# Turning the attention output of the last step on TensorE in place of a transposing DMA

## The chip, the core and the metric

The kernel runs on one core of a Trainium2 chip. The core has five engines that work side by side, each through its own list of instructions in order: TensorE (PE; its weight loads are shown apart as PEld), VectorE (DVE), ScalarE (ACT), GpSimd (POOL) and SyncE (SP), which here only issues DMAs. They meet through semaphores. The metric is the device time of one execution in microseconds (us), lower being better.

## What is computed

Attention for 4 batches, 8 heads, 768 positions and 64 elements a head, followed by a feed-forward layer with a maximum of three products:

```
scores = q @ k.T / sqrt(64)
mask   = causal                                   for retrieval heads
mask   = causal and (key < 4 or distance < 64)    for the others
a      = softmax(scores where mask else -1e9)
x      = (a @ v), its heads laid side by side     # 3072 x 512
h      = max(x @ w1, x @ w2, x @ w3)              # 3072 x 768
out    = h @ w_out                                # 3072 x 512
```

Inputs and output are float32; the kernel computes its products in float16 with float32 sums.

## The kernel before, in words

**Tiling.** The rows of a batch are cut into two halves of 384 positions. One step, t, is one batch, one half and one group of four heads (`qd`): 4 x 2 x 2 = 16 steps, t = 0 to 15, with `where(t)` giving batch, half and group. Step 15 is the last: batch 3, second half, heads 4 to 7. A step has two pairs of heads, i = 0 and 1.

**Stages of a step.** `scores` multiplies q and k into PSUM (line 441) and takes the exponential on ScalarE (line 452); `masks` multiplies by the mask, mostly on POOL. `av(t, i)` multiplies the result with v for one pair: 60 small products for the two pairs of a second-half step, 30 each (line 495), into one PSUM bank `oacc`. VectorE then takes the reciprocal of the sums (line 503) and scales into `x`, float16, positions on partitions (line 505). The feed-forward layer needs this turned, features on partitions: tile `xT[b, half][hp]`, hp being the pair's number from 0 to 3 in its batch.

**Two ways to turn x.** Which one a step takes is told by the tuple `BY_DMA` (line 89):

- If t is in it, `av` itself issues a transposing DMA on SP's queue from x to xT (line 514), right after x is made.
- If not, `av` keeps x, and a later call `turn_x(t, i)` transposes its three 128 x 128 blocks on TensorE into a PSUM bank named `tr` (line 527) and copies that to xT, on VectorE unless told otherwise (line 531).

In both cases `turn_x` of a half's last pair puts the feed-forward of that half into `queue`. Before the change steps 0, 1 and 3 are turned by TensorE, all others by DMA.

**The feed-forward** `ffn(b, half)` is a generator that hands out lots of work. There are 18 lots of four products of 384 columns (line 338: three weights for each of six output blocks), each followed by a copy on ScalarE (line 346) or a maximum on VectorE (line 349), the third maximum writing `hT`; and then, for each of three row blocks, six products with `w_out` (line 364), a copy out of PSUM (line 370), and a DMA of the result (line 371). A row block counts for two turns of the generator. Results of products sit in a ring of four PSUM banks (`bkp`, one bank each for `yy`, `oacc` and `tr`); the last feed-forward takes every second one from the pool of `scores` instead (named `yst`).

**What sets the order.** The order is written out by hand (`ctx.enter_context(tc.manual_schedule())`). The list `PROGRAM` has one row for each part of a step's scores: a number of lots of feed-forward to weave in, a flag, and four strings of calls; the loop at its end runs the first string, the scores, the second string, about half of the lots by `fill`, the third string, the rest of the lots, and the fourth string. Its last three rows, for which no scores are left, are

```
(3.94, False, "v 15 1 ap", "x 14 1", "", "av 15 0, x 15 0"),
(3.94, False, "", "av 15 1", "", ""),
(3.94, False, "x 15 1", "", "", ""),
```

where `av 15 0` is `av(15, 0)` and `x 15 0` is `turn_x(15, 0)`. Thus `x 15 0` directly follows `av 15 0` with nothing woven between, `av 15 1` comes next, and `x 15 1` follows the lots that are woven in after it. When the list ends, the last feed-forward runs alone.

Of the kernel before, what the change touches and what calls it, by code (L numbers as in the profile page):

```python
# [51 lines left out]
def kernel(  # L52
# [33 lines left out]
    NQ = H // G  # L86
    NT4 = B * 2 * NQ

    BY_DMA = (2, 4, 5, 6, 7, 8, 9, 10, 11, 12, 13, 14, 15)

    consts = ctx.enter_context(tc.tile_pool(name="consts", bufs=1))
    stage = ctx.enter_context(tc.tile_pool(name="stage", bufs=3))
# [390 lines left out]
    def av(t, i):  # L483
# [25 lines left out]
        if hp == 0:  # L509
            xT[b, half] = [  # L510
                xtp.tile([P, HB, P], FP16, tag=f"xT{n}", name=f"xT{n}") for n in range(KS)
            ]
        if t in BY_DMA:
            nc.sync.dma_start(
# [5 lines left out]
    def turn_x(t, i, op=None):  # L520
        b, half, qd = where(t)
        hp = 2 * qd + i
        if t not in BY_DMA:
            x = xs.pop((t, i))
# [202 lines left out]
```

## Time and profile before

| what | value |
|---|---|
| median of 6 runs | 202.04 us (201.52 to 202.25) |
| profiled execution | 201.88 us |
| its span (first to last instruction recorded) | 200.0 us |
| TensorE busy | 188.7 us (94%) |
| VectorE busy | 123.2 us (62%) |
| ScalarE busy | 131.6 us (66%) |
| POOL busy | 122.5 us (61%) |
| transposing DMAs, line 514 | 26, median 2.4 us from issue to landing |
| turns by TensorE, line 527 | 18 blocks, 0.22 us each, overlapping |
| copies of turned blocks by VectorE, line 531 | 4, median 0.34 us |

A row of the timeline gives the start in us from the span's start, the length, the engine, the line, the operation with output and input, and how many instructions are merged into it; in square brackets stands how long the engine sat idle before it and whose result ended the wait. Matmuls overlap, so a row's length is that of the whole group, and one product alone shows a longer time than its share of a group. A row of the chain of work that ended last gives start, length and what held the chain.

### The profile page before, as it was taken

The page shows a single profiled execution, that of the slowest core. Times are in us where ns is not written, and L with a number is a line of the kernel's source. Part 1 is how long each engine was busy: PE and PEld are TensorE (multiplying, and loading weights), DVE is VectorE, ACT ScalarE, POOL GpSimd, SP SyncE. Part 2 cuts the span into 40 slices and gives each one's busy share as a digit, 9 for nine tenths or more (in the row PEclk, how much of TensorE's full clock was granted, in tenths as well). Part 3 has the DMA queues.
Part 4 walks back from the last instruction along what each step waited for, and adds up shares of the span by engine and source line. Part 5 has one row for each costly group of instructions (what it writes and reads, how often), then busy time and mean ns, then how long its engine had stood idle before and what let it go on. Part 6 is the DMA issues. An engine that isn't in the chain of part 4 may idle for free.

```text
span 200.0 us, 5133 instructions
## 1 busy us (share of the span) xinstructions
PE 188.7 (94%) x2059; PEld 109.0 (55%) x2059; DVE 123.2 (62%) x242; ACT 131.6 (66%) x206; POOL 122.5 (61%) x153
## 2 busy tenths in 40 slices
PE   7797998896999999999999999999999999999992
PEld 2355654454566466574555565575555565755552
DVE  2798687999777839871554649961555234443540
ACT  4586798597875777666787685848768769313221
POOL 3599169479896905787969635699947547500000
PEclk9999999999999999999999999999999999999999
DMA  6999999997729892804359995502401240023004
GB/s 182 269 222 245 278 236 214 209 211 177 174 52 167 161 260 94 169 11 141 98 90 142 176 247 126 100 20 86 134 20 23 105 75 20 3 57 141 3 0 157
DMA packets 43245, 26.48 MB, mean 132 GB/s; under 512 B 33558, under 2 KB 38230, under 8 KB 43222
## 3 DMA queue, kind: packets, MB, share of 16 engines
q1 hardware_dynamic: 37206, 15.01, 34.4%
q0 software_dynamic: 4784, 10.23, 26.3%
q10 hardware_dynamic: 1232, 0.92, 1.4%
q8 instruction: 16, 0.26, 0.6%
q14 instruction: 7, 0.06, 0.1%
HBM read 25.17 MB, written 6.29 MB: 157 GB/s over the span
## 4 chain that ended last, share of the span: by engine, by line
PE 74%; DMA 10%; POOL 6%; DVE 3%; issue 2%; ACT 2%; SPq 1%; DVEq 0%; ACTq 0%; POOLq 0%
PE yy L338 39%; PE yy L364 13%; PE st L441 10%; PE oacc L495 9%; DMA vs<-in_v_dram 6%; PE yst L338 3%; DMA ks<-in_k_dram 2%; DVE KQ L190 2%; ACT pt L452 1%; DMA out_dram<-ot 1%; POOL vs L208 1%; POOL qs L126 1%; POOL ks L126 1%; PE yst L364 1%; ACT ot L370 1%
## 5 line engine op out<-in xcount | busy, mean ns | idle before, releaser
L479 POOL TENSOR_TENSOR pt<-pt,mk 128x512 f16<-128x512 f16 (+1 forms) x76 | 80.4, 1081 | 37.2 <-ACT pt L452 37.1
L452 ACT ACTIVATE pt<-st 128x1024 f16<-128x1024 f32 (+3 forms) x99 | 83.1, 894 | 21.1 <-PE st L441 20.3
L349 DVE TENSOR_TENSOR acc<-yy,acc 128x384 f16<-128x384 f32 x45 | 25.1, 558 | 28.1 <-PE yy L338 18.4
L338 PE MATMUL yy<-xT,w2t 128*128 128x384 f16 x180 | 35.9, 327 | 1.7 <-DVE hT L349 1.7
L338 PE MATMUL yy<-xT,w1t 128*128 128x384 f16 x180 | 36.1, 327 | 0.1
L338 PE MATMUL yy<-xT,w0t 128*128 128x384 f16 x180 | 35.6, 326 | 0.4 <-DVE xT L531 0.4
L346 ACT CAST acc<-yy 128x384 f16<-128x384 f32 x45 | 21.0, 484 | 17.1 <-PE yy L338 10.6
L364 PE MATMUL yy<-woutt,hT 128*128 128x512 f16 (+1 forms) x138 | 32.0, 375 | 0.0
L441 PE MATMUL st<-KQ 32*128 32x384 f16 (+4 forms) x560 | 28.5, 279 | 0.6 <-DVE KQ L190 0.5
L349 DVE TENSOR_TENSOR hT<-yy,acc 128x384 f16<-128x384 f32 x45 | 24.9, 559 | 6.7 <-PE yy L338 4.3
L495 PEld LDWEIGHTS <-pt 128*128 128x128 f16 x672 | 23.9, 97 | 5.4 <-issue 2.2
L338 PEld LDWEIGHTS <-w2t 128*128 128x128 f16 x192 | 17.6, 98 | 15.2 <-issue 4.0
L190 DVE STREAM_TRANSPOSE KQ<-kq 128x384 f32<-128x384 f32 x24 | 25.7, 1131 | 0.0
L338 PEld LDWEIGHTS <-w0t 128*128 128x128 f16 x192 | 18.2, 98 | 12.9 <-issue 1.0
L495 PE MATMUL oacc<-va,pt 128*128 128x65 f16 x352 | 24.8, 193 | 0.3 <-ACT va L392 0.3
L338 PEld LDWEIGHTS <-w1t 128*128 128x128 f16 x192 | 17.3, 98 | 12.5 <-issue 1.3
L370 ACT COPY ot<-yy 128x512 f32<-128x512 f32 x22 | 12.9, 587 | 15.5 <-PE yy L364 9.3
L495 PE MATMUL oacc<-vf,pt 128*128 128x65 f16 x320 | 21.1, 193 | 0.9 <-POOL vf L394 0.9
L364 PEld LDWEIGHTS <-hT 128*128 128x128 f16 x150 | 13.9, 98 | 14.5 <-issue 0.3
L441 PEld LDWEIGHTS <-KQ 32*128 32x128 f16 (+1 forms) x560 | 12.2, 93 | 17.3 <-issue 11.8
L505 DVE TENSOR_TENSOR x<-oacc,rc 128x384 f16<-128x384 f32 x32 | 17.8, 557 | 1.3 <-DVE rc L503 0.2
L503 DVE RECIPROCAL rc<-oacc 128x6 f32<-128x6 f32 x32 | 6.1, 191 | 20.1 <-PE oacc L495 19.8
(71 smaller groups left out, 129.0 us busy)
## 6 DMA issues: line engine op xcount, KB each, us to landing
out_dram<-ot SPq DMA_DIRECT2D x23, 256.0 KB, 2.9
vs<-in_v_dram SPq DMA_DIRECT2D x21, 256.0 KB, 6.0
kq<-in_k_dram POOLq DMA_DIRECT2D x6, 384.0 KB, 5.4
kq<-in_q_dram POOLq DMA_DIRECT2D x6, 384.0 KB, 7.6
qs<-in_q_dram ACTq DMA_DIRECT2D x4, 192.0 KB, 3.8
ks<-in_k_dram SPq DMA_DIRECT2D x4, 192.0 KB, 3.6
w0t<-in_moe_w_dram POOLq DMA_DIRECT2D x1, 768.0 KB, 7.4
ks<-in_k_dram POOLq DMA_DIRECT2D x2, 384.0 KB, 6.8
```

The costliest lines, as they stand in the source:

```text
L190: nc.vector.transpose(out=dst.rearrange("c (p j) -> c j p", j=n)[:, j0:j1], in_=src.rearrange("c (j i) -> c j i", i=R),)
L338: nc.tensor.matmul(yy[:, 0:HALF], w_t[wi][:, ks, ni * P : (ni + 1) * P], xT[b, half][ks].rearrange("p a t -> p (a t)"), start=(ks == 0), s ...
L346: nc.scalar.copy(out=acc[ni], in_=yy[:, 0:HALF])
L349: nc.vector.tensor_tensor(out=dst, in0=yy[:, 0:HALF], in1=acc[ni], op=ALU.max)
L364: nc.tensor.matmul(yo[:, 0:n], hT[ns][:, tb * P : (tb + 1) * P], woutt[:, ns, c : c + n], start=(ns == 0), stop=(ns == NNB - 1),)
L370: op(out=ot[:, c : c + n], in_=yo[:, 0:n])
L441: nc.tensor.matmul(sts[g // m][:, g % m, c0 : c0 + n * P], KQ[rows, 0, ki * P : (ki + 1) * P], KQ[rows, 1, t0 : t0 + n * P], start=(c0 == ...
L452: nc.scalar.activation(out=pts[t, i][:, u, h0 : h0 + m, 0:w], in_=st[:, :, 0:w], func=AF.Exp, scale=sc,)
L479: engine.tensor_tensor(out=x, in0=x, in1=m, op=ALU.mult)
L495: nc.tensor.matmul(o[:, qi, hl, 0 : D + 1], pt[:, u, hl, c : c + P], vv[:, 2 * hp + hl, ki, 0 : D + 1], start=(idx == 0), stop=(idx == len ...
L503: nc.vector.reciprocal(out=rc, in_=o[:, :, :, D])
L505: nc.vector.tensor_tensor(out=x, in0=o[:, :, :, 0:D], in1=rc.unsqueeze(3).to_broadcast([P, HB, 2, D]), op=ALU.mult,)
```

## The change

The step t = 15 is taken out of `BY_DMA`. Its two transposing DMAs are no longer issued, and the two calls `turn_x(15, 0)` and `turn_x(15, 1)`, which until now did nothing on TensorE for this step, turn x there and copy it to xT on VectorE. The rows of `PROGRAM` stay as they are.

```diff
-    BY_DMA = (2, 4, 5, 6, 7, 8, 9, 10, 11, 12, 13, 14, 15)
+    BY_DMA = (2, 4, 5, 6, 7, 8, 9, 10, 11, 12, 13, 14)
```

The code on which it acts, unchanged, in `av` and in `turn_x`:

```
        if t in BY_DMA:
            nc.sync.dma_start(out=xT[b, half][hp], in_=x.rearrange(...), transpose=True)
        else:
            xs[t, i] = x
...
        if t not in BY_DMA:
            x = xs.pop((t, i))
            tr = bank([P, 1024], FP16, "tr")
            for qi in range(HB):
                nc.tensor.transpose(tr[:, qi * P : (qi + 1) * P], ...)
            (op or nc.vector.tensor_copy)(out=xT[b, half][hp]..., in_=tr[:, 0:HALF])
```

## The prediction

> **What bounds the kernel now.** I read the page's span and its chain of work that ended last first, to know which engine sets the end:
>
> ```profile
> span 200.0 us, 5133 instructions
> PE 74%; DMA 10%; POOL 6%; DVE 3%; issue 2%; ACT 2%; SPq 1%; DVEq 0%; ACTq 0%; POOLq 0%
> ```
>
> TensorE holds three quarters of the chain. What matters is whether it holds it where the change is made, so next comes the chain in order of time, cut to 172 to 182 us (start, length, what), where the step of t = 15 lies:
>
> ```profile
> 171.97 1.79 PE yy L338 x11
> 173.76 1.87 PE oacc L495 x60
> 175.63 1.30 PE yy L338 x8
> 176.93 3.89 PE yy L364 x18
> 180.82 0.65 PE yst L338 x4
> ```
>
> Every piece begins where the one before it ends: no gap. The 60 products are the two calls av(15, 0) and av(15, 1). From there to the last product TensorE is the chain, at a granted clock of 1.00 in each stretch that I asked for. So any time that the change makes TensorE spend or wait there goes whole into the end.
>
> The third view is the timeline of the same moments. First TensorE's matmuls (start, length; lines left out are like their neighbours):
>
> ```profile
> 174.47 0.22 PE L495 MATMUL oacc<-va,pt 128*128 128x65 f16 x2
> 174.53 0.22 PE L495 MATMUL oacc<-vf,pt 128*128 128x65 f16 x2
> ...
> 175.47 0.81 PE L338 MATMUL yy<-xT,w1t 128*128 128x384 f16 x4
> 176.12 0.81 PE L338 MATMUL yy<-xT,w2t 128*128 128x384 f16 x4
> 176.77 4.05 PE L364 MATMUL yy<-woutt,hT 128*128 128x512 f16 x18
> 180.66 0.65 PE L338 MATMUL yst<-xT,w0t 128*128 128x384 f16 x3
> ```
>
> Counting 30 products from 173.60, the first call's last one is in the row at 174.47 and ends at 174.69; the second call starts at 174.53 with no pause. Then VectorE:
>
> ```profile
> 174.73 0.20 DVE L503 RECIPROCAL rc<-oacc 128x6 f32<-128x6 f32 x1 [0.95 <-PE oacc L495]
> 174.96 0.56 DVE L505 TENSOR_TENSOR x<-oacc,rc 128x384 f16<-128x384 f32 x1
> 175.67 0.20 DVE L503 RECIPROCAL rc<-oacc 128x6 f32<-128x6 f32 x1
> 176.10 0.56 DVE L505 TENSOR_TENSOR x<-oacc,rc 128x384 f16<-128x384 f32 x1 [0.23 <-DVE rc L503]
> 176.58 0.55 DVE L349 TENSOR_TENSOR acc<-yy,acc 128x384 f16<-128x384 f32 x1
> 177.23 0.56 DVE L349 TENSOR_TENSOR hT<-yy,acc 128x384 f16<-128x384 f32 x1
> ```
>
> x of (15, 0), what is to be turned, is ready at 174.96 + 0.56 = 175.52 us. While VectorE makes it, TensorE already runs the second call. That is the whole point of the case.
>
> Last, what a turn by TensorE costs, from steps that are turned so already (line 527), out of two stretches of the timeline:
>
> ```profile
> 15.68 0.33 PE L527 MATMUL tr<-ident,x 128*128 128x128 f16 x3
> ...
> 15.85 0.35 PE L495 MATMUL oacc<-va,pt 128*128 128x65 f16 x6
> ...
> 49.19 0.34 PEld L527 LDWEIGHTS <-x 128*128 128x128 f16 x6 [0.94 <-DVE x L505]
> 49.19 0.51 PE L527 MATMUL tr<-ident,x 128*128 128x128 f16 x6 [0.65 <-DVE x L505]
> ```
>
> Three turns hold TensorE from 15.68 to 15.85, 0.17 us; six in a row give (0.51 - 0.22)/5 = 0.058 us each, 0.22 being the length of one, so again 0.17 for three. The last two rows also show a turn waiting for x: the product that it waits for ended at 48.58 + 0.56 = 49.14 on VectorE, and the load began at 49.19, 0.05 us later.
>
> **What the Trainium skill says.** "TensorE: Matmul & The Clock Gate", Part 3, The mechanism: TensorE may pull weight loads ahead of products in flight, but the products start and end strictly in program order. The trace agrees where it can show it: the third call's products at 15.32 were held 0.29 us for ScalarE's copy of v, and the turn behind them, whose x had been ready since 14.46 + 0.56 = 15.02, did not go ahead; it ran at 15.68, after all of them. Same page, Part 4, PE-mode transpose: a 128x128 turn takes some 275 ns within a kernel, with its result in PSUM, to be copied out. The trace has 0.22 us for one and 0.058 us for each of a row, because they overlap; I use the trace. Same page, Why this matters for your kernels: gaps of TensorE over about 3 us lose the fast clock; the new gap is under 1 us, and after 0.65 us idle at 49.19 the trace's products of 384 columns ran at their usual pace.
>
> **The change, part by part.** (a) Removed: two transposing DMAs on SP's queue, begun at 175.59 and about 176.9. Their bytes moved until about 178.8, and the median from issue to landing over all 26 is 2.4 us. The first product that reads these xT tiles is at 180.66 and follows the one before it without a gap. Gain: 0. SP's next duty, the output at 178.93, waits for ScalarE (12.6 us, in SP's waits), not for these. The queue is never the limit, and the output is issued no earlier.
>
> (b) "x 15 0" stands right after "av 15 0" with no filling between, and "av 15 1" opens the next line. So TensorE's order becomes 30 products, 3 turns, 30 products. The turns cannot start before x: 175.52 + 0.05 = 175.57. The second call then starts at 175.57 + 0.17 = 175.74 in place of 174.53: +1.21 us, of which 0.17 is work and 1.04 is time in which TensorE used to do the second call's products. Behind the waiting turn stands everything that TensorE has left; no other engine has work to bring forward in this stretch (POOL ended at 172.5, ScalarE and VectorE only serve TensorE).
>
> (c) "x 15 1" stands after the fill that follows av(15, 1). Two lots of line 338 and one lot of line 364 (six products, 6 x 0.216 = 1.30 us) run first. Its turns come at 176.77 + 1.21 + 1.30 = 179.28; its x is ready at 176.66 + 1.21 = 177.87, so 1.4 us of cover hide the wait; uncovered, it would cost what (b) does, some 1.2. Three turns, again +0.17 us. The lots of line 364 are only regrouped, 6 and 12 rather than 18.
>
> (d) Two copies from PSUM on VectorE, 0.34 us each (line 531, median). The first runs at about 175.95 to 176.29, before the second reciprocal, due at 175.67 + 1.21 = 176.88: cover 0.59. The second ends near 180.0, and the first product that wants it is at 182.04: cover 2.0. Cost 0; without cover 0.34 each.
>
> (e) Two PSUM banks more in a ring of four. The first turn takes one free since 173.13, the second that of the second call, free at 177.87. The first lot of line 364 takes the first turn's (free 176.29, wanted 177.98); the next two take banks whose readers end by 179.00, wanted at 179.45 and later. The closest cover is 0.4 us. Cost 0; a late copy there would cost its lateness, at most about 0.3.
>
> (f) The loads of hT for line 364 are just in time today (0.33 us of idle weight loading, but 18 products in 4.05 us is (4.05 - 0.375)/17 = 0.216 each, the normal pace). All of that chain moves by the same 1.21, so nothing is added.
>
> Sum: 1.21 + 0.17 = 1.38 us. The profiled execution took 201.88 us (span 200.0 and 1.88 around it), so 203.26; the median of the runs is 0.16 higher, so 203.4.
>
> What the trace doesn't show is this turn between these two calls. Bounds: 0.34 us if the wait were hidden wholly (only six turns of work), 1.38 + 6 x (0.275 - 0.058) = 2.7 us if each turn took the skill's latency unoverlapped. No gain is in it, since (a) frees nothing. I take 1.38, since each piece has its row.
>
> **The rivals.** *The wait is filled* (not slower): TensorE starts the second call while the turn waits. Place: 174.69 to 175.57. Price: only 6 x 0.058 = 0.34 us, giving 202.4, within what can be told from no change. It decides if 0.94 us or more of the 1.21 is filled. For it: 30 independent products are queued. Against: they are behind the turn, and the wait at 15.32 was not filled by the ready turn behind it. *The removed DMAs paced the end*: their tiles could land late in ordinary runs, as one of 26 did after 7.8 us. It decides only if they land over 180.66 + 1.38 = 182.04, 5.1 us after the second issue; here bytes ended near 178.8. It would give 202.0 or less. *VectorE becomes late*: the copy in front of the second reciprocal loses its 0.59 us and pushes hT, which has no slack, by up to 0.34: 203.8. Against: the stall itself gives VectorE that room. *Turns at full latency*: 2.7 us, 204.7; against it stand the 18 turns of the trace. That the change does nothing is excluded: both the issue and the turn test the same list.
>
> **How the numbers follow.** Forecast 0.83; filled wait 0.05; late DMAs 0.02; late VectorE 0.06; full latency 0.04. Under 0.2%, 0.4 us, a change of this kernel cannot be told from none. Slower: 0.83 + 0.06 + 0.04 = 0.93; same 0.05; faster 0.02. The six runs spread over 0.73 us, so two medians can differ by 0.3 with no change; with 0.2 for the terms, and reaching up to the late VectorE, the range is 202.8 to 204.0.
>
> **What would show it.** Right: TensorE idle some 0.9 us before line 527 near 174.7, released by VectorE's x of line 505; the second call near 175.74; the turns of "x 15 1" with no idle ahead of them, after six products of line 364; the lot at 180.66 found at 182.04; a span near 201.4. Wrong: products of the second call ahead of the turns; a gap before the last FFN's first product in most runs of before; idle time of TensorE waiting for line 531 or a bank; turns spaced over 0.1 us.

## The result, and the profile after

The changed kernel takes 203.11 us (median of 35 runs) against 202.15 us for the kernel before (72 runs): ratio 1.0049, 95% interval 1.0039 to 1.0058, so 0.99 us slower (0.79 to 1.17). The forecast was slower, 203.4 us, by 1.38 us. The direction and the place are right; 0.4 us of the size are not. The profiled execution has a span of 201.4 us.

The chain of work that ended last in the changed kernel, in order of time around step 15 (start, length, what):

```profile
174.15 0.95 PE oacc L495 x30
...
175.12 0.21 DVE rc L503
...
175.35 0.57 DVE x L505
...
175.97 0.34 PE tr L527 x3
176.31 0.93 PE oacc L495 x30
177.24 1.30 PE yy L338 x8
178.54 1.29 PE yy L364 x6
179.84 0.17 PE tr L527 x3
180.01 2.59 PE yy L364 x12
182.60 0.65 PE yst L338 x4
```

The piece of 60 products is now two of 30, and between them the chain leaves TensorE for VectorE's reciprocal and scaling: what used to run beside the second call is on the path. The timeline of the changed kernel gives the waits:

```profile
175.35 0.56 DVE L505 TENSOR_TENSOR x<-oacc,rc 128x384 f16<-128x384 f32 x1
175.96 0.17 PEld L527 LDWEIGHTS <-x 128*128 128x128 f16 x3 [1.00 <-DVE x L505]
175.97 0.34 PE L527 MATMUL tr<-ident,x 128*128 128x128 f16 x3 [0.88 <-DVE x L505]
...
176.15 0.23 PE L495 MATMUL oacc<-vf,pt 128*128 128x65 f16 x2
...
176.35 0.36 DVE L531 COPY xT<-tr 128x384 f16<-128x384 f16 x1 [0.44 <-PE tr L527]
...
177.28 0.20 DVE L503 RECIPROCAL rc<-oacc 128x6 f32<-128x6 f32 x1 [0.57 <-PE oacc L495]
...
178.38 1.46 PE L364 MATMUL yy<-woutt,hT 128*128 128x512 f16 x6
...
179.68 0.33 PE L527 MATMUL tr<-ident,x 128*128 128x128 f16 x3
...
180.04 0.36 DVE L531 COPY xT<-tr 128x384 f16<-128x384 f16 x1 [0.82 <-PE tr L527]
...
182.43 0.81 PE L338 MATMUL yst<-xT,w0t 128*128 128x384 f16 x4
```

The first turn finds TensorE idle for 0.88 us; the second follows its products without a bracket. VectorE's copies end long before anything needs them.

To compare executions I cut each into three stretches: up to the first product of av(15, 0); from there to the end of VectorE's last copy (line 370); and from there to the end of the span. All times come from the traces, one profiled execution for each kernel.

| kernel | first product of av(15, 0) | middle stretch | last stretch | span |
|---|---|---|---|---|
| before | 173.60 | 23.29 | 3.10 | 199.98 |
| changed | 173.99 | 24.67 | 2.72 | 201.38 |

The middle grew by 1.38 us, as forecast. But the last stretch, where no line of the change lies, shrank by 0.37 (3.098 and 2.724 before rounding); and the first, also untouched, was 0.39 longer in this one execution. The last two cancel, so the span is 201.4 just as forecast, for a wrong reason: the first stretch varies from one execution to the next, and the shorter last one, as the experiments below show, comes back in every trace with the last signal at that place.

Where the first stretch gets its length can be seen. In the twelve traces of this study it ends between 173.50 and 174.65, and the kernels overlap: 173.58 to 174.43 in the five with both transposing DMAs of step 15, 173.50 to 174.65 in the five with neither. From the first product with the weights w1, near 23 us, to its end it takes 150.71 to 150.75 us in all twelve. So its length is settled in the first 24 us, far ahead of step 15. In the two executions compared it was the load of w1 from memory: it landed 8.4 us after its issue before, and 9.1 us after in the changed kernel, where TensorE waited for it. TensorE's weight loads of before and then of the changed kernel (timeline):

```profile
22.69 0.59 PEld L338 LDWEIGHTS <-w1t 128*128 128x128 f16 x4
```

```profile
23.23 0.44 PEld L338 LDWEIGHTS <-w1t 128*128 128x128 f16 x4 [0.64 <-DMA w1t<-in_moe_w_dram]
```

The last stretch comes next. Each DMA raises a semaphore, a counter, when its data has landed. SP ends the program with a row of single waits, one after the other, and only then begins the common close of all engines. These are SP's instructions on the kernel's last line, from the last landing on, of the kernel before:

```profile
L722 SPq EVENT_SEMAPHORE  x7: 28/28/28, 198.7 to 199.1; - x7
L722 SPq DRAIN  x2: 7/10/13, 199.2 to 199.2; - x2
```

and of the changed kernel:

```profile
L722 SPq EVENT_SEMAPHORE  x2: 28/28/28, 200.0 to 200.5; - x2
L722 SPq DRAIN  x2: 7/10/13, 200.5 to 200.6; - x2
```

Before, the last output's landing frees the wait at 198.72 and six more follow to 199.09, 0.061 us apart, before the drain at 199.15. In the changed kernel the wait that the landing frees, at 200.47, is the last one (the other of the two, at 200.00, belongs to the output before), and the drain follows 0.065 later. The records of the traces name the semaphores: DMAs issued by SP and ScalarE signal on eight of them in turn, and SP waits for these eight in a fixed order. Two DMAs fewer move the last output from the second of the eight to the last: 6 x 0.061 = 0.37 us less to do after it has landed. The last transfer itself was no quicker: from its issue to the wait that it frees it is 1.80 us before, 1.78 in the changed kernel, and 1.76 to 1.80 in all twelve traces.

### The profile page after: what moved, and what is told of

Read it like the earlier page. It is cut to its first block, busy times and chain, and to the rows that moved or that the text cites. A ratio compares the mean times of both kernels' runs of the same rounds, so it can differ in the third digit from the quotient of the medians.

```text
span 201.4 us, 5141 instructions
## 1 busy us (share of the span) xinstructions
PE 189.4 (94%) x2065; PEld 109.3 (54%) x2065; DVE 124.1 (62%) x244; ACT 131.6 (65%) x206; POOL 122.4 (61%) x153
## 4 chain that ended last, share of the span: by engine, by line
PE 75%; DMA 9%; POOL 6%; DVE 4%; issue 2%; ACT 2%; SPq 1%; DVEq 0%; ACTq 0%; POOLq 0%
PE yy L338 38%; PE yy L364 14%; PE st L441 9%; PE oacc L495 9%; DMA vs<-in_v_dram 7%; PE yst L338 3%; DMA ks<-in_k_dram 2%; DVE KQ L190 2%; ACT pt L452 1%; PE yst L364 1%; POOL vs L208 1%; DVE x L505 1%; POOL qs L126 1%; POOL ks L126 1%; POOL kn L139 1%
```

## The experiments

Theory A is just that: the sum of 1.38 us is right, and the place of the last signal takes off 0.37. Rival B: it is the transposing DMAs and their traffic, now missing, that give 0.4 us back. Rival C: TensorE's stall costs less over many runs than in the profile.

**Six small DMAs in the kernel before** move the last output's signal to the end of the row and change nothing else.

```diff
+    pads = [consts.tile([1, 2], FP16, name=f"pad{n}") for n in range(6)]
+    def small_dmas():
+        for x in pads:
+            nc.sync.dma_start(out=x, in_=zero[0:1, 0:2])
...
-        (3.94, False, "v 15 1 ap", "x 14 1", "", "av 15 0, x 15 0"),
+        (3.94, False, "v 15 1 ap", "x 14 1", "small", "av 15 0, x 15 0"),
```

> The kernel before with six more 4-byte DMAs on SP's queue, issued while SP waits for the first x of t = 15 anyway. DMAs from SP and ScalarE signal on eight semaphores in turn, and SP ends the kernel with one wait for each; six more DMAs put the last output's semaphore at the end of that row of waits, where the changed kernel has it. Theory A (the place of the last signal in the closing row of waits is worth 6 x 0.06 us): 0.37 us faster than before, about 201.8, ratio 0.998, and after the last landing only one wait is left. Theory B (the 0.4 us come from the missing transposing DMAs and their traffic): no faster than before, ratio 1.000 or a little over. Theory C (TensorE's stall costs less over many runs than in the profile): ratio 1.000.

Measured: 201.65 us, ratio 0.9974 (0.9961 to 0.9987), or 0.53 us faster (0.26 to 0.79). SP's row, from the landing before the last on:

```profile
L729 SPq EVENT_SEMAPHORE  x2: 28/28/28, 198.3 to 198.8; - x2
L729 SPq DRAIN  x2: 7/10/12, 198.9 to 199.0; - x2
```

The transposing DMAs are all there, and the time is gained all the same. B alone can't give this. The middle stretch is 23.28, the last 2.72. This kernel is the fastest of the study, ahead of both kernels compared.

**Eight small DMAs in the kernel before** (the same edit with 8) bring the semaphores round to where they were.

> Control for the cost of the small DMAs: eight of them, so that the semaphores come round to where they were. Theory A: as before, ratio 1.000, with six waits left after the last landing. Theory B and C: ratio 1.000 as well. If the small DMAs cost anything themselves it shows here.

Measured: 202.15 us, ratio 1.0005 (0.9986 to 1.0023), six waits left, last stretch 3.10. So neither the small DMAs nor their number pays, only the place.

**Two small DMAs in the changed kernel** (the same edit with 2) undo the move of the signal.

> The changed kernel with two small DMAs in place of the two transposing ones, so that the last output signals where it did before the change. Theory A: the whole 1.38 us of TensorE shows, ratio 1.0068, about 203.5, 0.37 above the changed kernel. Theory B and C: as the changed kernel, ratio 1.005.

Measured: 203.42 us, ratio 1.0047 (1.0034 to 1.0061). The profile fits A, with the row of before back and a last stretch of 3.07 us:

```profile
L729 SPq EVENT_SEMAPHORE  x7: 28/28/28, 200.1 to 200.5; - x7
```

The ratio does not: its interval leaves out A's 1.0068 and holds the 1.005 of B and C. So the kernel was run again, beside a control.

> The changed kernel with two small DMAs once more, beside the next one on the same chip, since its first ratio, 1.0047 (1.0034 to 1.0061), lies between the theories while its profile has six waits after the last landing and a last stretch of 3.07 us like before. Theory A: 1.0068 and 0.37 us above the changed kernel with eight small DMAs. Theory B or C: 1.005, and no difference to that kernel.

Measured: 203.42 us, ratio 1.0076 (1.0047 to 1.0105). Last stretch 3.08, middle 24.67.

**Eight small DMAs in the changed kernel**, the control.

> The changed kernel with eight small DMAs: the last output signals where it does in the changed kernel, at the end of the row of waits. Theory A, B and C: as the changed kernel, ratio 1.005, about 203.1. If the small DMAs cost time in this kernel, it is more.

Measured: 203.42 us, ratio 1.0075 (1.0046 to 1.0104), last stretch 2.70, middle 24.67. The total times of these two do not tell 0.37 us apart: with six runs each, the spread of the first stretch is as large (first product of av(15, 0) at 173.50 in one and 174.65 in the other, the load of w1 landing at 22.72 and 23.87). In total time this pair is inconclusive; only the stretches, which leave the early part out, separate them.

**The first turn moved later**, so that its wait is hidden.

```diff
-        (3.94, False, "v 15 1 ap", "x 14 1", "", "av 15 0, x 15 0"),
+        (3.94, False, "v 15 1 ap", "x 14 1", "", "av 15 0"),
...
-        (3.94, False, "x 15 1", "", "", ""),
+        (3.94, False, "x 15 0, x 15 1", "", "", ""),
```

> The changed kernel with x 15 0 moved from behind av 15 0 to beside x 15 1, so that its wait of 0.88 us has two lots of line 338 and one of line 364 to hide it. Forecast by the sum: 0.34 us of turns stay, the other 1.04 us go; with theory A's 0.37 it comes to 0.03 us under before, ratio 1.000, and no idle time of TensorE at line 527. Theory C: less than 1.04 us is gained, ratio 1.001 to 1.003.

Measured: 202.32 us, ratio 1.0001 (0.9983 to 1.0020). TensorE's timeline:

```profile
177.58 1.48 PE L364 MATMUL yy<-woutt,hT 128*128 128x512 f16 x6
178.89 0.50 PE L527 MATMUL tr<-ident,x 128*128 128x128 f16 x6
179.23 1.03 PE L364 MATMUL yy<-woutt,hT 128*128 128x512 f16 x4
```

Six turns in a row, none waiting, take the place from 178.89 to 179.23, 0.34 us. The middle stretch is 23.64, 0.35 over before; the last 2.72. So 1.04 of the 1.38 were the stall: moving the call wins it back. The total time alone does not exclude C here, whose 1.001 to 1.003 lies in part inside the interval.

**One pair at a time.** The test in `av` and `turn_x` also looks at the pair; seven small DMAs stand in for the six, since one transposing DMA less moves the signal by one.

```diff
+    BY_PE = ((15, 0),)            # and ((15, 1),) in the other kernel
-        if t in BY_DMA:
+        if (t in BY_DMA) and (t, i) not in BY_PE:
-        if t not in BY_DMA:
+        if t not in BY_DMA or (t, i) in BY_PE:
```

> Only the first pair of t = 15 is turned by TensorE, the second stays with its DMA; seven small DMAs keep the last output's semaphore at the end of the row. The sum gives +1.21 us for the stall and its turns and theory A takes off 0.37: +0.84, ratio 1.0042, TensorE idle 0.88 us at the first turn. If the stall cost less over many runs (theory C), below 1.003.

Measured: 203.17 us, ratio 1.0050 (1.0033 to 1.0067). Its first turn in the timeline:

```profile
176.07 0.34 PE L535 MATMUL tr<-ident,x 128*128 128x128 f16 x3 [0.88 <-DVE x L513]
```

Middle stretch 24.50, so +1.21 as forecast; last 2.71. C's "below 1.003" lies just outside the interval, so C falls here, by total time.

> Only the second pair is turned by TensorE, with seven small DMAs. The sum gives +0.17 us for three turns without a wait, theory A takes off 0.37: -0.20, ratio 0.999. Theory B, where a missing transposing DMA is worth some 0.2 and the semaphores nothing: ratio 1.000.

Measured: 202.13 us, ratio 0.9991 (0.9975 to 1.0006). Middle 23.46, so +0.17 as forecast; last 2.69. The ratio can't exclude B's 1.000, the stretches fit A.

**Other places in the row**, each executed once: three and seven small DMAs in the kernel before.

> The kernel before with three small DMAs: the last output's semaphore is the fifth of the eight in the closing row. Theory A: three waits of 0.06 us left after the last landing, and the stretch from the end of VectorE's last copy to the end of the span is 3.09 - 3 x 0.061 = 2.91 us. Theory B: 3.09, as in the kernel before.

> The kernel before with seven small DMAs: the last output's semaphore is the first of the eight. Theory A: seven waits left after the last landing, and a last stretch of 3.09 + 0.06 = 3.15 us, the longest of all. Theory B: 3.09.

Measured last stretches: 2.92 us with three and 3.16 us with seven. The total times of these single executions, 202.54 and 201.93 us (before in the same round 202.03), say nothing about A, since their first stretches end at 174.43 and 173.58. The whole row is thus

| small DMAs added to before | waits left after the last landing | last stretch, us |
|---|---|---|
| 6 | 0 | 2.72 |
| 3 | 3 | 2.92 |
| none (8) | 6 | 3.10 (3.10) |
| 7 | 7 | 3.16 |

(3.16 - 2.72) / 7 = 0.063 us for each wait left. A holds at every place measured; nothing in B makes the last stretch follow the number of DMAs modulo eight.

## Why the prediction was right, and where it was not

- **Bound.** TensorE set the end from step 15 on: the middle stretch grew by 1.38 us, and nothing absorbed any of it.
- **(b), the stall.** Confirmed: +1.21 us alone, as forecast, of which moving the call wins back 1.04. The turn began 0.05 to 0.06 us after x (175.91 and 175.96), and the second call 0.18 after that, at 176.15. The order of products held: none of the 30 queued ones slipped ahead of the waiting turn, as the Trainium skill's page "TensorE: Matmul & The Clock Gate", Part 3, The mechanism, says of products. So the rival of the filled wait is out.
- **(c), the second turn.** +0.17 us, no wait. The x of the second pair was ready at 178.07, the turns came at 179.68.
- **(d), (e), (f), the covers.** None was used up. The first copy ended at 176.71, the second reciprocal began at 177.28: 0.57 against 0.59. TensorE waits neither for line 531 nor for a bank in this stage, so late VectorE is out; the turns stayed 0.058 us apart, so full latency is out as well.
- **(a), the removed DMAs.** This step failed. It asked whether the DMAs' landing or SP's queue held anyone up, and both answers were right: no one waited. (One reading was not: the 12.6 us stand before the output at 194.51; the output at 178.93 waited 0.6 us for ScalarE.) In all five traces that have both DMAs the middle stretch is 23.28 to 23.29 us, so they never came late there, and the rival of DMAs that paced the end is out. But the step didn't count that a DMA issue also takes a turn among the semaphores, and so sets how many of SP's closing waits stand behind the last output. The term put at 0 is -0.37 us. With it the sum is 1.38 - 0.37 = 1.01 us, against 0.99 (0.79 to 1.17) measured.
- **Forecast span.** That 201.4 was met is luck: a longer first stretch made up for the shorter last one in that execution. It is no support for the sum of 1.38; the middle stretch is.

What stays open: the six small DMAs gave 0.53 us where the stretches give 0.37; the interval (0.26 to 0.79) holds both. In the changed kernel the place of the last signal is shown by the stretches alone: in total time the first run with two small DMAs came out below A's 1.0068 (1.0034 to 1.0061), the second held it, and two and eight small DMAs were not told apart.

## What to carry to other kernels

A turn by the engine that sets the pace costs little if its input is ready, and the wait for it as well if it is not: here 0.17 us against 1.21 us for three blocks, decided by whether independent products stand between the product and its turn. When a change adds or removes a DMA, follow its semaphore too, to the very end of the program, and not only its bytes. Compare executions by stretches that leave a noisy start out: here the middle stretch of one kernel agreed within 0.01 us from trace to trace, the last one for the same place of the signal within 0.04, while the total times of the kernel before ran from 201.40 to 203.34 us.

## What the runs showed that was not expected

SP's closing waits cost about 0.06 us each even when their DMAs had landed long before, so that the place of the last output's semaphore in that row is worth up to 0.44 us (2.72 to 3.16 us in the last stretch). Six 4-byte DMAs, issued while the queue was waiting anyway, made the kernel before faster (ratio 0.9974); eight of them did not (1.0005), so it is the shift in count that pays.

TensorE's first product with w1, at 22.8 to 23.9 us, and the start of step 15 lie 150.71 to 150.75 us apart in all twelve traces. So nearly all of the scatter up to there comes from the first 24 us.
